# A decode kernel whose second FFN matrix is loaded on 96 + 32 partitions without repeated rows

## The chip, the cores and the metric

The kernel runs on one core of a Trainium2 chip. The metric is the device time of one execution in microseconds (us); smaller is better. A core has a tensor engine (PE, with its weight loads listed as PEld), a vector engine (DVE), a scalar engine (ACT), GpSimd (POOL), and a queue engine (SP) that does nothing but ask for transfers. Data lie in HBM, are moved by 16 DMA engines into SBUF (128 partitions), and matrix products arrive in PSUM (128 partitions, 8 banks of 512 float32 each).

## What is computed

One decode step for two sequences (B = 2, one token each), all in bfloat16: cached attention with 32 heads of 128 over 4096 keys, and beside it a feed-forward network (FFN) with a ReLU; a gate mixes the two.

```python
def reference(A_x, A_k_cache, A_v_cache, A_wq, A_wo, B_x, B_w1, B_w2, gate_w):
    x = A_x                                                  # [2, 1, 512]
    g = sigmoid((x * gate_w).sum(-1, keepdims=True))
    q = heads(x @ A_wq)                                      # 32 heads of 128
    scores = einsum("bhqd,bhkd->bhqk", q, A_k_cache) * 128 ** -0.5
    o = einsum("bhqk,bhkd->bhqd", softmax(scores), A_v_cache)
    a = merge(o) @ A_wo                                      # [2, 1, 512]
    h = maximum(einsum("bsd,df->bsf", x, B_w1), 0)           # w1 [512, 1376]
    b = einsum("bsf,fd->bsd", h, B_w2)                       # w2 [1376, 512]
    return g * a + (1 - g) * b
```

K and V have 64 MB each, `wq` and `wo` 4 MB each, `w1` and `w2` 1.4 MB each. Every byte is used once.

## The kernel before

**Queues and order.** The order of each engine's instructions is written out by hand: `pe(...)`, `dve(...)`, `act(...)`, `pool(...)` and `sp(...)` append an instruction to an engine's list; `waits` name the marks of other instructions (`signal`), `dwaits` a transfer's semaphore. All large loads go through SP, one after another, onto one queue: `w1` (line 264), `wq` (265), ten segments of K (269), V in seven units and two halves (274, 277, 280), `wo` in two parts (282, 283) and `w2` in six (284 and 288). SP waits ahead of an issue until the buffer that it fills is free.

**The stages.** `gate` transposes x, which then lies in `xT3` as [128, 4, 2] (partition p holds the elements 4p to 4p+3 of the 512), and works out the gate; `gm` is 1 - g. `q_proj` makes q with x at rest: `xTw` is the stationary operand, 32 columns wide, and `wq` moves, 512 columns at a time, in four column groups of the array (`tile_position=(0, 32 * (n % 4))`), so that results lie on the partitions 0, 32, 64 and 96 of the banks 5 and 6 (line 331). `ffn_h` follows. Then 64 pieces of K pass through `k_turn` (a block transposition of 32x32 on the DVE, line 384, into one of three buffers of `kt`) and `k_scores` (lines 405 and 197). `softmax` and `spread` make the weights; `v_unit` multiplies with V (line 458), `v_extract` and `o_gather` collect the heads.

**h.** `ffn_h` (line 363) makes h with w1 at rest: 44 matmuls (11 tiles of 128 columns of w1, 4 parts of the sum), each loading a 128x128 piece of w1 as weights and moving the 2 columns of x. Tile ft < 10 takes every tenth column of the first 1280, so that h number 10 p + ft comes to partition p, and tile 10 takes the columns 1248 to 1375. Two DVE instructions (line 373) apply the ReLU and the gate and write `hT` [128, 11, 2]. The first 32 entries of tile 10 are there twice, so POOL sets them to zero (line 377). `w1` lies in the memory of the first buffers of `kt`, and the first `k_turn` waits for the last of these matmuls.

**w2.** `w2f` is [128, 5632] in bfloat16, 11 rows of 512 for each partition. Row r < 10 on partition p is row 10 p + r of w2 (line 235); row 10 holds the rows 1248 to 1375, 32 of which are loaded twice (line 284). The five pieces of line 288 are column ranges of the rest: rows 0 to 4, 5 to 7, 8, and the two halves of 9. They go to the memory of the softmax's `E`, so the first of the six waits until the last `spread` is over.

**The end.** `project` multiplies with `wo` (line 504) in four column groups; the sums of the groups are copied by the DVE into `YW` (line 507). `fin(g)` is where the end result grows, 2 rows of 128 columns in each of the four column groups. `ffn_f(10, first=True)` starts this sum; `wo_sum` (line 526) adds the attention's part; `ffn_f(0)` to `ffn_f(8)` (line 512) add h times w2 row by row, each waiting for its piece of w2; `ffn_last(9)` does the last row with its weights already loaded (lines 202 and 208). DVE and ACT copy the result out (564, 566), and SP and ACT send it (291).

Of the kernel before, what the change touches and what calls it, by code (L numbers as in the profile page):

```python
# [3 lines left out]
dt = mybir.dt  # L4
# [6 lines left out]
DFF = 1376  # L11
# [74 lines left out]
def bass_gated_mix__gqa_block_cached__dense_activation_relu__decode_kernel(  # L86
# [14 lines left out]
    sb = nc.alloc_sbuf_tensor  # L101
# [4 lines left out]
    xT3 = sb("xT3", [128, 4, 4], dt.bfloat16)  # L106
# [26 lines left out]
    O_sb = sb("O_sb", [32, 2, 128], dt.bfloat16)  # L133
    oW = sb("oW", [128, 32, 2], dt.bfloat16)
    hT = sb("hT", [128, 11, 2], dt.bfloat16)
    out_sb = sb("out_sb", [2, 512], dt.bfloat16)


# [2 lines left out]
    w1 = flat[:, 0:2752].bitcast(dt.bfloat16)  # L141
    E = flat[:, 0:2048].bitcast(dt.bfloat16)
    ET = flat[:, 4096:6144].bitcast(dt.bfloat16)
    w2f = flat[:, 0:2816].bitcast(dt.bfloat16)
    w2 = w2f.rearrange("p (r n) -> p r n", n=512)
# [5 lines left out]
    PSF = nc.alloc_psum_tensor("PS", [128, 4096], dt.float32)  # L151
    PSB = PSF[:, :].bitcast(dt.bfloat16)

    def psf(p0, p1, c0, n):
        return PSF[p0:p1, c0:c0 + n]

    BANK = 512
    QR_B = 5
# [8 lines left out]
    H_C0 = MISC + 72  # L167
# [7 lines left out]
    sem = {n: nc.alloc_semaphore("sem_" + n) for n in names}  # L175
# [12 lines left out]
    def adder(engine):  # L188
        def add(fn, waits=(), signal=None, dwaits=()):
            P.add(engine, fn, waits=[marker(w) for w in waits], signal=marker(signal) if signal else None, dwaits=dwaits)  # L190
        return add

    pool, dve, act, pe, sp = (adder(e) for e in ("pool", "dve", "act", "pe", "sp"))
# [7 lines left out]
    def load_at(e, weights, g):  # L201
        return e.add_instruction(mybir.InstLdweights(
            tile_size=(128, 32), tile_position=(0, 32 * g), name=nc.get_next_instruction_name(), engine=mybir.EngineType.PE,
            ins=[e.lower_ap(weights)], outs=[]))

    def held_at(e, out, lhsT, rhs, g):
        low = e.lower_ap
        return e.add_instruction(mybir.InstMatmult(  # L208
            start_tensor_calc=False, stop_tensor_calc=True, tile_size=(128, 32), tile_position=(0, 32 * g), ldweights=False,
            name=nc.get_next_instruction_name(), engine=mybir.EngineType.PE, ins=[low(rhs), low(lhsT)], outs=[low(out)]))  # L210
# [5 lines left out]
         waits=["c_i16z"], signal="c_i16")  # L216
# [5 lines left out]
         waits=["c_i32z"], signal="c_i32")  # L222
# [6 lines left out]
         waits=["c_s4z"], signal="c_s4")  # L229
# [2 lines left out]
    wq_in = A_wq.rearrange("(p t) n -> p (t n)", t=4)  # L232
    w1_in = B_w1.rearrange("(p t) f -> p (t f)", t=4)
    wo_in = A_wo.rearrange("(p r) n -> p (r n)", r=32)
    w2_in = B_w2[0:1280, :].rearrange("(p r) n -> p (r n)", r=10)
    k_rows = A_k_cache.rearrange("b h s d -> (b h s) d")
    v_rows = A_v_cache.rearrange("b h s d -> (b h s) d")

# [20 lines left out]
    def place(g):  # L259
        return (4, 0, 2)[g % 3]  # L260
# [5 lines left out]
    for g, (u, halves) in enumerate(segments):  # L266
        dst = kv[:, 4, :] if len(halves) == 1 else region[:, place(g) // 2, :]
        src = unit_in(k_rows, u)[:, 16384 * halves[0]:16384 * (halves[-1] + 1)]
        sp(lambda e, g=g, dst=dst, src=src: e.dma_start(dst, src).then_inc(sem_k[g % 3], 16),
           waits=([f"kt_{last_of[g - 3]}"] if g >= 3 else ["pe_qr1"] if g == 2 else []))  # L270
    for u in range(7):
        if u == 2:
            for hf, dst, w in ((0, kv[:, 4, :], "kt_63"), (1, kv[:, 0, :], "pe_v_0")):
                sp(lambda e, hf=hf, dst=dst: e.dma_start(dst, unit_in(v_rows, 2)[:, 16384 * hf:16384 * (hf + 1)]).then_inc(sem_v[2 - 2 * hf], 16),
                   waits=[w])
            continue
        sp(lambda e, u=u: e.dma_start(region[:, u % 2, :], unit_in(v_rows, u)).then_inc(sem_v[u % 2], 16),
           waits=([f"pe_v_{u - 2}"] if u >= 2 else [f"kt_{last_of[7]}"] if u == 0 else [f"kt_{last_of[8]}"]))
    for hf in range(2):
        sp(lambda e, hf=hf: e.dma_start(kv[:, 2 + hf, :], unit_in(v_rows, 7)[:, 16384 * hf:16384 * (hf + 1)]).then_inc(sem_v[1 + hf], 16),  # L280
           waits=(["pe_v_5"] if hf == 0 else []))
    sp(lambda e: e.dma_start(wo_sb[:, 0:12288], wo_in[:, 0:12288]).then_inc(sem["wo0"], 16), waits=["pe_v_2"])
    sp(lambda e: e.dma_start(wo_sb[:, 12288:16384], wo_in[:, 12288:16384]).then_inc(sem["wo1"], 16))
    sp(lambda e: e.dma_start(w2[:, 10, :], B_w2[1248:1376, :]).then_inc(sem["w2a"], 16),
       waits=[f"pt_7_{hq}" for hq in range(4)])

    for name, c0, c1 in (("w2b", 0, 2560), ("w2c", 2560, 4096), ("w2d", 4096, 4608), ("w2e", 4608, 4864), ("w2f", 4864, 5120)):
        sp(lambda e, name=name, c0=c0, c1=c1: e.dma_start(w2f[:, c0:c1], w2_in[:, c0:c1]).then_inc(sem[name], 16))

    def send(b):  # L290
        return lambda e: e.dma_start(out.rearrange("b s n -> (b s) n")[b:b + 1, :], out_sb[b:b + 1, :]).then_inc(sem["out"], 16)
# [69 lines left out]
                waits=(["pe_q", "c_qbuf"] if g < 2 else [f"pe_sc_{last_of[g - 2]}"]), signal=f"q_{g}_{hq}")  # L361

    def ffn_h():
        for ft in range(11):
            for t in range(4):
                def fn(e, ft=ft, t=t):
                    o = t * DFF
                    cols = w1[:, o + ft:o + 1280:10] if ft < 10 else w1[:, o + 1248:o + 1376]
                    return e.matmul(psf(0, 128, H_C0 + 2 * ft, 2), lhsT=cols, rhs=xT3[:, t, 0:2], start=(t == 0), stop=(t == 3))
                pe(fn, dwaits=([(sem["w1"], 16)] if ft == 0 and t == 0 else []),  # L370
                   signal=("pe_h" if ft == 10 and t == 3 else None))
        for b in range(2):
            dve(lambda v, b=b: v.tensor_scalar(out=hT[:, :, b], in0=PSF[:, H_C0 + b:H_C0 + 22:2], scalar1=0.0,
                                               scalar2=gm[:, b:b + 1], op0=ALU.max, op1=ALU.mult),
                waits=["pe_h", "dve_gm"], signal=f"dve_h{b}")

        pool(lambda g: g.memset(hT[0:32, 10, :], 0.0), waits=["dve_h0", "dve_h1"], signal="c_h10")

    def k_turn(i):
        g, u, hf, h, rr = pieces[i]  # L380
# [116 lines left out]
    def fin(g):  # L497
        return psf(32 * g, 32 * g + 2, FIN_B * BANK, 128)

    def project():  # L500
        for r in range(32):
            dw = [(sem["wo0"], 16)] if r == 0 else [(sem["wo1"], 16)] if r == 24 else []
            t = r % 4
            pe(lambda e, r=r, t=t: e.matmul(psf(32 * t, 32 * t + 2, WO_B * BANK, 512), lhsT=oW[:, r, :], rhs=wo_sb[:, 512 * r:512 * r + 512],  # L504
                                            start=(r < 4), stop=(r >= 28), tile_position=(0, 32 * t)),
               dwaits=dw, waits=(["dve_oW0", "dve_oW1", "dve_z"] if r == 0 else []), signal=("pe_wo" if r == 31 else None))
        dve(lambda v: v.tensor_copy(out=YW, in_=psf(0, 128, WO_B * BANK, 512)), waits=["pe_wo"], signal="dve_yw")

    def ffn_f(r, first=False, signal=None):
        dw = {10: [(sem["w2a"], 16)], 0: [(sem["w2b"], 16)], 5: [(sem["w2c"], 16)], 8: [(sem["w2d"], 16)]}.get(r, [])  # L510
        for g in range(4):
            pe(lambda e, g=g: e.matmul(fin(g), lhsT=hT[:, r, :], rhs=w2[:, r, 128 * g:128 * g + 128],
                                       start=first, stop=(signal is not None), tile_position=(0, 32 * g)),
               dwaits=(dw if g == 0 else []), waits=(["dve_h0", "dve_h1", "c_h10", "dve_z"] if first and g == 0 else []),
               signal=(signal if g == 3 else None))

    def ffn_last(r):
        for g in range(4):
            pe(lambda e, g=g: load_at(e, hT[:, r, :], g))
        for g in range(4):  # L520
            pe(lambda e, g=g: held_at(e, fin(g), hT[:, r, :], w2[:, r, 128 * g:128 * g + 128], g),
               dwaits=([(sem["w2f" if g else "w2e"], 16)] if g % 2 == 0 else []), signal=(f"pe_fin{g // 2}" if g % 2 else None))

    def wo_sum():
        for g in range(4):
            pe(lambda e, g=g: e.matmul(fin(g), lhsT=selw[:, :], rhs=YW[:, 128 * g:128 * g + 128],
                                       start=False, stop=False, tile_position=(0, 32 * g)),
               waits=(["dve_yw", "dve_selw0"] if g == 0 else []))

    gate()  # L530
    selectors()
# [1 line left out]
    q_put(0)  # L533
    q_put(1)
    ffn_h()
    for i in range(64):
        k_turn(i)
# [15 lines left out]
            o_gather(0, [3])  # L553
    o_gather(1, [0, 1, 2, 3])
    project()
    ffn_f(10, first=True)
    wo_sum()
    for r in range(9):
        ffn_f(r)
    ffn_last(9)  # L560
    for c in range(4):
        dst, src = out_sb[:, 128 * c:128 * c + 128], fin(c)
        if c % 2 == 0:
# [36 lines left out]
```

## Time and profile before

| | |
|---|---|
| time, median of 3 runs | 344.48 us (344.44 to 344.49) |
| the profiled execution | 344.46 us |
| its span in the profile | 343.2 us |
| PE / PEld / DVE / ACT / POOL busy | 58 / 16 / 51 / 7 / 6% of the span |
| read from HBM | 145.46 MB, 424 GB/s over the span |
| `ffn_h` on PE (line 369) | 2.56 us from 22.67 us on |
| first transposition of K (line 384) | 25.91 us |
| `project` on PE (line 504) | 3.17 us from 335.05 us on |
| last matmul, sends | 340.9 to 341.2 us, 341.8 us |

The span is what the profiler records between the first and the last instruction; the execution's time has 1.3 us more around it. The profile gives for each engine the busy time, for each source line the instructions with their mean duration and what ended the idle time before them, for the DMA queues the packets and bytes, and a chain of waits: the work that ended last, followed back step by step to what released it. "DMA share" is the mean busy share of the 16 DMA engines.

### The profile page before, as it was taken

To read this page: it belongs to the slowest core of one execution; us is meant where nothing else is said; L and a number is where in the kernel's file an instruction comes from. 1 tells how busy PE (TensorE), PEld (TensorE's weight loads), DVE (VectorE), ACT (ScalarE), POOL (GpSimd) and SP (SyncE) were. 2 spreads that over 40 slices of the span, in tenths; PEclk is the share of its full clock that TensorE was granted. 3 is DMA by queue.
4 is the path that set the end of the run, shared out by engine and by line. 5 is a ranking of instruction groups with operands and counts; after the bars stand their busy time and mean duration, and the time that the engine had idled before them with its cause. 6 is when DMAs were issued, how large, how long until landed. Compare 5 with 4: busy or idle time off the path is not lost.

```text
span 343.2 us, 2528 instructions
## 1 busy us (share of the span) xinstructions
PE 200.1 (58%) x1226; PEld 53.4 (16%) x970; DVE 176.6 (51%) x124; ACT 22.8 (7%) x70; POOL 19.6 (6%) x34
## 2 busy tenths in 40 slices
PE   0167429799969799699799337423080503306455
PEld 0141001111111111111111012200030201102121
DVE  2239059899789899698999562202001030201021
ACT  1040000000000000000000240000000000000000
POOL 8000000000000000000000041101000010100000
PEclk9985858999989999989999856865558575856568
DMA  8998989899998999998999989999999999899996
GB/s 348 428 489 369 481 374 481 378 477 428 422 489 367 429 443 466 392 466 382 475 428 428 468 382 424 441 466 413 443 413 445 435 420 474 384 420 443 428 400 236
DMA packets 4340, 145.61 MB, mean 424 GB/s; under 512 B 485, under 2 KB 1002, under 8 KB 1258
## 3 DMA queue, kind: packets, MB, share of 16 engines
q1 hardware_dynamic: 4322, 145.46, 98.5%
q8 instruction: 8, 0.13, 0.2%
q14 instruction: 2, 0.02, 0.0%
q10 hardware_dynamic: 8, 0.00, 0.0%
HBM read 145.46 MB, written 0.00 MB: 424 GB/s over the span
## 4 chain that ended last, share of the span: by engine, by line
DMA 67%; DVE 19%; PE 11%; ACT 1%; issue 1%; POOL 0%; SPq 0%; DVEq 0%
DMA kv<-in_A_k_cache_dram 31%; DMA kv<-in_A_v_cache_dram 19%; DVE kt L384 16%; DMA kt<-in_B_w_dram 12%; PE PS L458 7%; DMA kv<-in_A_wq_dram 4%; ACT kt L426 1%; PE PS L405 1%; PE PS L197 1%; PE PS L331 1%; DVE mpad L411 1%; DVE kt L468 1%; POOL ptm L440 0%; DVE qbuf L464 0%; DVE kt L430 0%
## 5 line engine op out<-in xcount | busy, mean ns | idle before, releaser
L384 DVE STREAM_TRANSPOSE kt<-kv 128x2048 f32<-128x2048 f32 x64 | 141.2, 2274 | 22.7 <-DMA kv<-in_A_k_cache_dram 22.7
L405 PE MATMUL PS<-kt,qbuf 128*128 128x512 bf16 x256 | 107.0, 418 | 30.4 <-DVE kt L384 25.3
L197 PE MATMUL PS<-kt,qbuf 128*128 128x512 bf16 x256 | 106.5, 416 | 0.0
L458 PE MATMUL PS<-kv,ptm 128*32 128x512 bf16 x512 | 48.7, 559 | 77.3 <-DMA kv<-in_A_v_cache_dram 73.8
L464 DVE TENSOR_TENSOR qbuf<-PS,maskc 128x512 f32<-128x512 f32 x8 | 5.5, 692 | 111.4 <-PE PS L458 111.4
L405 PEld LDWEIGHTS PS<-kt,qbuf 128*128 128x128 bf16 x256 | 25.8, 101 | 139.9 <-issue 71.4
L458 PEld LDWEIGHTS PS<-kv,ptm 128*32 128x32 bf16 x512 | 18.7, 131 | 106.0 <-issue 85.4
L440 POOL COPY ptm<-kt 32x512 bf16<-32x512 bf16 x16 | 11.2, 697 | 259.2 <-DVE rsum L472 175.9
L358 ACT ACTIVATE qbuf<-PS 32x8 bf16<-32x8 bf16 x40 | 7.8, 196 | 134.3 <-PE PS L197 133.0
L444 ACT ACTIVATE ptm<-kt 32x512 bf16<-32x512 bf16 x8 | 5.1, 653 | 90.0 <-PE PS L458 88.7
L468 DVE TENSOR_REDUCE kt<-qbuf 128x128 f32<-128x512 f32 x8 | 8.2, 1029 | 0.3
L426 ACT ACTIVATE kt<-PS,negm 128x512 bf16<-128x512 f32 x8 | 5.4, 697 | 30.4 <-DVE negm L422 30.4
L331 PE MATMUL PS<-kv,xTw 128*32 128x512 bf16 x32 | 3.6, 631 | 5.9 <-DMA kv<-in_A_wq_dram 5.9
L475 PE MATMUL PS<-rsum,sell 128*32 128x1 f32 x4 | 0.4, 197 | 10.1 <-DVE rsum L472 10.1
L430 DVE STREAM_TRANSPOSE kt<-kt 128x1024 bf16<-128x1024 bf16 x4 | 5.0, 1245 | 1.7 <-ACT kt L426 1.4
L346 DVE CAST qrow<-PS 128x256 bf16<-128x256 f32 x2 | 2.4, 1397 | 6.4 <-PE PS L331 6.4
L298 PE MATMUL PS<-ident,x_sb 3*128 3x3 bf16 x4 | 0.3, 166 | 6.2 <-DMA x_sb<-in_gate_w_dram 6.2
L504 PE MATMUL PS<-kv,oW 128*2 128x512 bf16 x32 | 3.2, 570 | 0.9 <-DMA kv<-in_A_wo_dram 0.9
L566 ACT ACTIVATE out_sb<-PS 2x128 bf16<-2x128 f32 x2 | 0.5, 270 | 45.8 <-PE PS L208 45.7
L301 DVE COPY xT<-PS 128x12 bf16<-128x12 bf16 x1 | 0.2, 169 | 6.5 <-PE PS L298 6.5
L230 POOL MEMSET ptm<- 128x4096 bf16 x1 | 3.5, 3502 | 0.0
L411 DVE TENSOR_REDUCE mpad<-PS 128x1 f32<-128x2048 f32 x1 | 2.3, 2293 | 2.2 <-PE PS L197 2.2
(64 smaller groups left out, 44.2 us busy)
## 6 DMA issues: line engine op xcount, KB each, us to landing
kv<-in_A_k_cache_dram SPq DMA_DIRECT2D x4, 4096.0 KB, 31.6
kv<-in_A_v_cache_dram SPq DMA_DIRECT2D x4, 4096.0 KB, 27.3
kv<-in_A_wq_dram SPq DMA_DIRECT2D x1, 4096.0 KB, 15.0
kv<-in_A_wo_dram SPq DMA_DIRECT2D x1, 3072.0 KB, 39.3
kt<-in_B_w_dram SPq DMA_DIRECT2D x1, 1376.0 KB, 5.8
kv<-in_A_wo_dram SPq DMA_DIRECT2D x1, 1024.0 KB, 41.3
kt<-in_B_w_dram SPq DMA_DIRECT2D x1, 640.0 KB, 42.0
kt<-in_B_w_dram SPq DMA_DIRECT2D x1, 384.0 KB, 42.4
```

The costliest lines, as they stand in the source:

```text
L197: return e.add_instruction(mybir.InstMatmult(start_tensor_calc=start, stop_tensor_calc=stop, tile_size=(128, 128), tile_position=(0, 0), l ...
L331: pe(lambda e, n=n, t=t: e.matmul(psf(32 * (n % 4), 32 * (n % 4) + 32, (QR_B + n // 4) * BANK, 512), lhsT=xTw[:, t, :], rhs=wq_sb[:, t, n ...
L358: act(lambda a, hq=hq: a.activation(out=qbuf[32 * hq:32 * hq + 32, g % 2, :, :, 32 + 32 * hq], in_=cols[32 * hq:32 * hq + 32, u4 // 2, 2 * ...
L384: dve(lambda v: v.transpose(out=dst, in_=pairs[:, h, 64 * rr:64 * rr + 64]), waits=([f"pe_sc_{i - NKT}"] if i >= NKT else ["pe_h"] if i == ...
L405: return e.matmul(args[0], lhsT=args[1], rhs=args[2], start=first, stop=last)
L411: dve(lambda v: v.tensor_reduce(out=mpad[:, 0:1], in_=psf(0, 128, 0, 2048), axis=AX.X, op=ALU.max), waits=["pe_sc_63", "c_mpad"], signal=" ...
L426: act(lambda a, bk=bk, e2=e2: a.activation(out=blocks[:, bk, :, 16 * e2:16 * e2 + 16], in_=psf(0, 128, bk * BANK, 512).rearrange("p (r n) ...
L440: pool(lambda e, args=args: e.tensor_copy(**args), waits=waits, signal=f"pt_{u}_{hq}")
L444: act(lambda e, args=args: e.activation(func=ACT.Copy, **args), waits=waits, signal=f"pt_{u}_{hq}")
L458: pe(lambda e, m=m, t=t, at=at: e.matmul(psf(32 * t, 32 * t + 32, V_B[u % 2] * BANK, 512), lhsT=ptm[:, u % 2, 4 * m:4 * m + 4, :, :], rhs= ...
L464: dve(lambda e: e.tensor_tensor(out=Y.rearrange("p (c d) -> p c d", c=4), in0=psf(0, 128, V_B[u % 2] * BANK, 512).rearrange("p (c d) -> p ...
L468: dve(lambda e: e.tensor_reduce(out=X2[:, u, :], in_=Y.rearrange("p (c d) -> p d c", c=4), axis=AX.X, op=ALU.add), waits=[f"dve_y{u}"], si ...
```

## The change

h is made with x at rest and w1 moving; w2 is loaded with no row twice. The partitions 0 to 95 hold 11 rows of w2 each (1056 rows), the partitions 96 to 127 hold 10 each (320 rows).

`ffn_h` issues 16 matmuls: for each of the 4 parts of the sum, four column groups, each moving 352 columns of w1 (320 in the last group). Group g's result lies on the partitions 32 g and 32 g + 1 of bank 5. One block transposition on the DVE reads [128, 352] from PSUM, sees it as 11 blocks of 32 columns (every eleventh column to a block), and writes `hrow` [128, 11, 32], where partition p holds h number 11 p + r for both sequences. The two ReLU instructions read `hrow`. The memset on POOL is gone.

Of w2, the first load puts the ten rows of the partitions 96 to 127 in place; the other five load the partitions 0 to 95: rows 5 to 10, 2 to 4, 1, and the two halves of row 0. The sum now begins with `wo_sum`, and the rows follow from 10 (on 96 partitions) down to 0.

```diff
+    hrow = sb("hrow", [128, 11, 32], dt.float32)
...
-    w2_in = B_w2[0:1280, :].rearrange("(p r) n -> p (r n)", r=10)
+    w2_in = B_w2[0:1056, :].rearrange("(p r) n -> p (r n)", r=11)
+    w2_in2 = B_w2[1056:1376, :].rearrange("(p r) n -> p (r n)", r=10)
...
-    sp(lambda e: e.dma_start(w2[:, 10, :], B_w2[1248:1376, :]).then_inc(sem["w2a"], 16),
+    sp(lambda e: e.dma_start(w2f[96:128, 0:5120], w2_in2).then_inc(sem["w2a"], 16),
        waits=[f"pt_7_{hq}" for hq in range(4)])
-    for name, c0, c1 in (("w2b", 0, 2560), ("w2c", 2560, 4096), ("w2d", 4096, 4608), ("w2e", 4608, 4864), ("w2f", 4864, 5120)):
-        sp(lambda e, name=name, c0=c0, c1=c1: e.dma_start(w2f[:, c0:c1], w2_in[:, c0:c1]).then_inc(sem[name], 16))
+    for name, c0, c1 in (("w2b", 2560, 5632), ("w2c", 1024, 2560), ("w2d", 512, 1024), ("w2e", 0, 256), ("w2f", 256, 512)):
+        sp(lambda e, name=name, c0=c0, c1=c1: e.dma_start(w2f[0:96, c0:c1], w2_in[:, c0:c1]).then_inc(sem[name], 16))
...
     def ffn_h():
-        for ft in range(11):
-            for t in range(4):
-                def fn(e, ft=ft, t=t):
-                    o = t * DFF
-                    cols = w1[:, o + ft:o + 1280:10] if ft < 10 else w1[:, o + 1248:o + 1376]
-                    return e.matmul(psf(0, 128, H_C0 + 2 * ft, 2), lhsT=cols, rhs=xT3[:, t, 0:2], start=(t == 0), stop=(t == 3))
+        for t in range(4):
+            for g in range(4):
+                def fn(e, g=g, t=t):
+                    n = 11 if g < 3 else 10
+                    cols = w1[:, t * DFF + 352 * g:t * DFF + 352 * g + 32 * n].rearrange("p (a r) -> p a r", r=n)
+                    dst = psf(32 * g, 32 * g + 2, QR_B * BANK, 352).rearrange("p (a r) -> p a r", r=11)[:, :, 0:n]
+                    return e.matmul(dst, lhsT=xT3[:, t, 0:2], rhs=cols, start=(t == 0), stop=(t == 3), tile_position=(0, 32 * g))
...
+        dve(lambda v: v.transpose(out=hrow[:, :, :], in_=psf(0, 128, QR_B * BANK, 352).rearrange("p (a r) -> p r a", r=11)),
+            waits=["pe_h"], signal="dve_hr")
         for b in range(2):
-            dve(lambda v, b=b: v.tensor_scalar(out=hT[:, :, b], in0=PSF[:, H_C0 + b:H_C0 + 22:2], scalar1=0.0,
+            dve(lambda v, b=b: v.tensor_scalar(out=hT[:, :, b], in0=hrow[:, :, b], scalar1=0.0,
                                                scalar2=gm[:, b:b + 1], op0=ALU.max, op1=ALU.mult),
-                waits=["pe_h", "dve_gm"], signal=f"dve_h{b}")
-        pool(lambda g: g.memset(hT[0:32, 10, :], 0.0), waits=["dve_h0", "dve_h1"], signal="c_h10")
+                waits=["dve_hr", "dve_gm"], signal=f"dve_h{b}")
...
-        dw = {10: [(sem["w2a"], 16)], 0: [(sem["w2b"], 16)], 5: [(sem["w2c"], 16)], 8: [(sem["w2d"], 16)]}.get(r, [])
+        dw = {10: [(sem["w2a"], 16), (sem["w2b"], 16)], 4: [(sem["w2c"], 16)], 1: [(sem["w2d"], 16)]}.get(r, [])
+        k = 96 if r == 10 else 128
         for g in range(4):
-            pe(lambda e, g=g: e.matmul(fin(g), lhsT=hT[:, r, :], rhs=w2[:, r, 128 * g:128 * g + 128],
+            pe(lambda e, g=g: e.matmul(fin(g), lhsT=hT[0:k, r, :], rhs=w2[0:k, r, 128 * g:128 * g + 128],
...
-    ffn_f(10, first=True)
     wo_sum()
-    for r in range(9):
+    for r in range(10, 0, -1):
         ffn_f(r)
-    ffn_last(9)
+    ffn_last(0)
```

More of the change, by code (lines that the diff above doesn't have):

```diff
@@ L363, in ffn_h @@
     def ffn_h():
-        for ft in range(11):
-            for t in range(4):
-                def fn(e, ft=ft, t=t):
-                    o = t * DFF
-                    cols = w1[:, o + ft:o + 1280:10] if ft < 10 else w1[:, o + 1248:o + 1376]
-                    return e.matmul(psf(0, 128, H_C0 + 2 * ft, 2), lhsT=cols, rhs=xT3[:, t, 0:2], start=(t == 0), stop=(t == 3))
-                pe(fn, dwaits=([(sem["w1"], 16)] if ft == 0 and t == 0 else []),
-                   signal=("pe_h" if ft == 10 and t == 3 else None))
+        for t in range(4):
[5 more added lines that the diff above has]
+                    return e.matmul(dst, lhsT=xT3[:, t, 0:2], rhs=cols, start=(t == 0), stop=(t == 3), tile_position=(0, 32 * g))
+                pe(fn, dwaits=([(sem["w1"], 16)] if g == 0 and t == 0 else []),
+                   signal=("pe_h" if g == 3 and t == 3 else None))
+        dve(lambda v: v.transpose(out=hrow[:, :, :], in_=psf(0, 128, QR_B * BANK, 352).rearrange("p (a r) -> p r a", r=11)),
+            waits=["pe_h"], signal="dve_hr")
         for b in range(2):
-            dve(lambda v, b=b: v.tensor_scalar(out=hT[:, :, b], in0=PSF[:, H_C0 + b:H_C0 + 22:2], scalar1=0.0,
+            dve(lambda v, b=b: v.tensor_scalar(out=hT[:, :, b], in0=hrow[:, :, b], scalar1=0.0,
                                                scalar2=gm[:, b:b + 1], op0=ALU.max, op1=ALU.mult),
-                waits=["pe_h", "dve_gm"], signal=f"dve_h{b}")
-        pool(lambda g: g.memset(hT[0:32, 10, :], 0.0), waits=["dve_h0", "dve_h1"], signal="c_h10")
+                waits=["dve_hr", "dve_gm"], signal=f"dve_h{b}")
     def k_turn(i):
@@ L507, in project, with ffn_f @@
         dve(lambda v: v.tensor_copy(out=YW, in_=psf(0, 128, WO_B * BANK, 512)), waits=["pe_wo"], signal="dve_yw")
-    def ffn_f(r, first=False, signal=None):
-        dw = {10: [(sem["w2a"], 16)], 0: [(sem["w2b"], 16)], 5: [(sem["w2c"], 16)], 8: [(sem["w2d"], 16)]}.get(r, [])
+    def ffn_f(r):
+        dw = {10: [(sem["w2a"], 16), (sem["w2b"], 16)], 4: [(sem["w2c"], 16)], 1: [(sem["w2d"], 16)]}.get(r, [])
+        k = 96 if r == 10 else 128
         for g in range(4):
[L512 to L515, printed above, removed]
+            pe(lambda e, g=g: e.matmul(fin(g), lhsT=hT[0:k, r, :], rhs=w2[0:k, r, 128 * g:128 * g + 128],
+                                       start=False, stop=False, tile_position=(0, 32 * g)),
+               dwaits=(dw if g == 0 else []), waits=(["dve_h0", "dve_h1"] if r == 10 and g == 0 else []))
     def ffn_last(r):
@@ L526, in wo_sum @@
             pe(lambda e, g=g: e.matmul(fin(g), lhsT=selw[:, :], rhs=YW[:, 128 * g:128 * g + 128],
-                                       start=False, stop=False, tile_position=(0, 32 * g)),
-               waits=(["dve_yw", "dve_selw0"] if g == 0 else []))
+                                       start=True, stop=False, tile_position=(0, 32 * g)),
+               waits=(["dve_yw", "dve_selw0", "dve_z"] if g == 0 else []))
     gate()
```

## The prediction, made before the result was known

> **What bounds the kernel now.** I read the page first: the share of the DMA queues beside that of the engines.
>
> ```profile
> span 343.2 us, 2528 instructions
> ...
> PE 200.1 (58%) x1226; PEld 53.4 (16%) x970; DVE 176.6 (51%) x124; ACT 22.8 (7%) x70; POOL 19.6 (6%) x34
> ...
> q1 hardware_dynamic: 4322, 145.46, 98.5%
> q8 instruction: 8, 0.13, 0.2%
> ```
>
> No engine is busy for more than 58% of the span; the one queue that carries every load keeps the 16 DMA engines busy for 98.5% of it. So the end comes when the last byte has come, plus a short tail. The chain of waits, in order of time, shows which bytes these are:
>
> ```profile
> 297.88 42.44 DMA kt<-in_B_w_dram
> ...
> 340.36 0.34 PE PS L512 x12
> ...
> 340.73 0.23 PE PS L512 x4
> 340.96 0.20 PE PS L208 x2
> ...
> 341.18 0.28 DVE out_sb L564
> ```
>
> The pieces of w2 are asked for 42 us ahead and stand in the queue behind V and wo; L512 takes each piece as it lands. This is the stage that the change rebuilds. Two more views of it: the DMA answer for 337.0 to 343.2 us, in 40 slices of 0.155 us,
>
> ```profile
> DMA  9999999999978566545464300000000000000000
> GB/s 363 476 390 390 377 423 443 363 403 330 420 258 301 218 244 238 221 169 182 169 182 139 103 0 0 0 0 0 0 0 0 0 0 0 0 7 7 0 0 0
> ```
>
> and a table of windows of one microsecond, whose last two columns are the DMA share and GB/s:
>
> ```profile
> 338.00:339.00 1.00, 0.28 (x10) 0.00 (x0) 0.69 (x1) 0.00 (x0) 0.00 (x0) 1.00 0.94 346
> 339.00:340.00 1.00, 0.85 (x28) 0.37 (x28) 0.00 (x0) 0.00 (x0) 0.00 (x0) 1.00 0.58 215
> 340.00:341.00 1.00, 0.61 (x18) 0.25 (x20) 0.00 (x0) 0.00 (x0) 0.00 (x0) 1.00 0.27 82
> ```
>
> The rate does not stop at once: it sinks from about 420 GB/s to 100 between 338.6 and 340.5 us. Some of the 16 engines have finished their share while others are still at it; the idle part of 338 to 341 us is 0.06 + 0.42 + 0.73 = 1.2 us per engine on the mean, so the first and the last are some 1.5 to 2 us apart. A likely reason, inferred only, is the q8 row: 8 fetches of 16 KB of program, 0.2% of 16 engines' span, which is 11 us or about 1.4 us each, each holding up one engine.
>
> **The change, part by part.**
>
> *Fewer bytes and packets.* Before, w2 comes as 1280 + 128 = 1408 rows of 1 KB, 32 of them twice; after as 1056 + 320 = 1376. That is 32 KB less. The rate of this stretch: L512 starts on r = 0 at 339.44 us (w2b is there) and on r = 5 at 340.36 (w2c, 384 KB): 393 KB (thousands) in 0.92 us, 427 GB/s. So the bytes are worth 0.08 us. The small pieces are dearer per byte: w2d, 128 KB, comes 0.37 us after w2c where 427 GB/s would take 0.31; 0.06 us more for 128 packets, 8 to an engine. After the change, w2 is 32 + 5 x 96 = 512 packets, before 768: 16 fewer to each engine, so 2 x 0.06 = 0.12 us, taken as 0.10 because the big pieces show less. Sum: **-0.18 us**, on the path that sets the end.
>
> *Where the bytes go.* Every large load of the trace goes to all 128 partitions. In the new order w2a puts 320 KB into partitions 96 to 127 alone, and then w2b to w2f put 1056 KB into 0 to 95 alone. The trace shows no load of this kind, so I bound it. Lower bound: the rate doesn't depend on the partitions, and it costs nothing. Upper bound: a partition takes no more than the trace ever gives one, 438 GB/s (the window from 100 to 200 us) over 128, 3.42 GB/s. Then w2a takes 10,240 B / 3.42 = 2.99 us in place of 328 KB / 438 = 0.75, so 2.24 more; w2b to w2f take 11,264 / 3.42 = 3.29 us in place of 1081 KB / 438 = 2.47, so 0.82 more; together **+3.06 us**. That holds if all engines do w2a together and then w2b together. But they are 1.5 to 2 us apart here: while the late ones fill 96 to 127, the early ones already fill 0 to 95, and what overlaps isn't lost, since the two parts together fill every partition evenly (10 and 11 KB). Taking off the 1.5 us leaves **+1.55 us**, and that is the value I take, because nothing in the trace shows a partition that takes data faster and the out-of-step end is plain to see.
>
> [...]
>
> *The tail behind the last byte.* L512 for r = 10 ran under the DVE copy L507 (338.28 to 338.97 us); now it comes behind `wo_sum` and the landing of w2b. Twenty of these matmuls took 0.45 us (339.44 to 339.89), so six rows take 0.54 us, and 288 KB of w2c after it need 288 x 1.024 / 427 = 0.69 us: hidden. Rows 4 to 2 take 0.27 us against 0.23 us for the 96 KB of w2d, 0.04 over, gone again by w2f. If PE were always late, it would cost 0.1 us. `ffn_last`, the copies and the sends stay as they are: 0.
>
> *h.* These are rows of the timeline, and one of L331, which has the new form (x at rest, four column groups) for q:
>
> ```profile
> 16.23 3.64 PE L331 MATMUL PS<-kv,xTw 128*32 128x512 bf16 x32 [5.91 <-DMA kv<-in_A_wq_dram]
> ...
> 22.67 2.56 PE L369 MATMUL PS<-xT,kt 128*128 128x2 bf16 x44
> ...
> 25.91 8.89 DVE L384 STREAM_TRANSPOSE kt<-kv 128x2048 f32<-128x2048 f32 x4 [0.28 <-DMA kv<-in_A_k_cache_dram]
> ```
>
> 44 matmuls and 2.56 us go. 16 come, of 352 columns: 3.64 / 32 x 16 = 1.82 us at most, 1.25 scaled by columns, so h is there at 24.0 to 24.6 us instead of 25.2. The block transposition is new on the DVE: 128x32 took 0.21 us (L413) and 128x2048 2.27 us (L384), so 128x352 is 0.21 + 320 x 2.06 / 2016 = 0.54 us; reading PSUM with a stride could make it as slow as the cast L346, 1.40 us for 256 elements, 1.9 us. The two L373 keep their 0.37 (they began at 25.27). The DVE is free for the first L384 at 24.9 to 26.9 us, against 25.9 when K lands: 0 to 1.0 us late. What hides even the 1.0: L384 releases the next K issue (L269), and 8 MB of K took 30.7 us from issue to landing where 433 GB/s needs 19.4, so 11 us of other loads stand ahead. Without that cover it would cost up to 1.0 us. The POOL memset L377 (0.09 us) and its wait go, worth nothing, as nothing near waited. SP's issues stay six for w2 with the same single wait.
>
> Sum: 344.46 us (this execution; its span of 343.2 and 1.3 around it; the median of the runs is 344.48) - 0.18 + 1.55 + 0 + 0 = 345.83, so **345.9 us**.
>
> **Rivals.**
>
> *A, the partitions don't matter* (not slower): 344.46 - 0.18 = 344.3 us. For it: each of the 16 engines runs at 438 / 16 = 27 GB/s whatever it loads, and nothing in this trace shows that the far side sets that. Against it: nothing shows more than 3.42 GB/s into a partition either, and w2a at full rate asks for 427 / 32 = 13. It decides if w2b lands no later than before.
>
> *B, in step, or on fewer engines*: the 32 rows queue up in full, +3.06 - 0.18, 347.3 us. A spread of w2a over 4 engines gives the same, since 328 KB at 4 x 27 GB/s is 3.0 us. For it: of two engines held up equally the shift doesn't help. Against it: the sinking rate above. [...]
>
> *C, fewer instructions*: 28 matmuls with their weight loads fewer on PE, 56 instructions, may save one of the 8 program fetches. If that were the one that the last engine waits for, the end would come up to 1.4 us sooner: 342.9 us with the bytes. Against it: the other fetches leave other engines equally late, so one saved moves nothing.
>
> **How the numbers follow.** About 0.2% (0.7 us) is what a measurement of this kernel can tell from no change. The forecast, the overlap leaving 0.9 to 2.4 us of the 3.06 (345.2 to 346.7 us), has 0.55; B 0.16; A 0.24; C 0.05. Slower is the forecast and B, 0.71; same is A, 0.24; faster is C, 0.05. The range from 344.2 to 347.2 us takes in A, whose chance is too large to leave out, and leaves out C and the top of B. The forecast's own range is 345.2 to 346.7.
>
> **What would show it.** Right: bytes read fall by 32 KB and the packets by some 256; in the last 5 us the GB/s fall well under 420 while DMA share stays high, from the landing of wo on; w2b lands 1 us or more later; L512 for r = 10 waits on the DMA for it; everything before 335 us stands where it did within 0.3 us; h is ready at or before 25.9 us. Wrong: the GB/s hold at 420 up to the sinking end (A); a first L384 later than 26.9 us, or a gap in the DMA row before 300 us (the cover is gone); or late landings of V or wo, which the change doesn't touch.

## The result, and the profile after

The changed kernel takes 347.19 us (median of 6 runs, 346.87 to 347.27), the kernel before 344.49 us (344.44 to 344.64): a ratio of 1.0076, interval 1.0065 to 1.0086, 2.70 us slower. The profiled execution took 346.96 us, its span 345.7.

The pages, the lines that count what the queue moved. First one line of the kernel before, then the changed kernel:

```profile
DMA packets 4340, 145.61 MB, mean 424 GB/s; under 512 B 485, under 2 KB 1002, under 8 KB 1258
```

```profile
span 345.7 us, 2472 instructions
...
DMA packets 4084, 145.58 MB, mean 421 GB/s; under 512 B 485, under 2 KB 778, under 8 KB 970
...
q1 hardware_dynamic: 4066, 145.43, 98.4%
q8 instruction: 8, 0.13, 0.2%
```

The change does what it says: 256 packets fewer (4340 before) and 0.03 MB less on q1 (145.46 before). The queue is as busy as ever, and the span is 2.5 us longer. The end of the chain of waits, changed kernel (start, duration, what):

```profile
298.13 44.05 DMA kt<-in_B_w_dram
342.18 0.14 issue
342.31 1.24 PE PS L518 x31
343.55 0.13 PE PS L209 x2
343.68 0.03 issue
343.70 0.28 DVE out_sb L568
```

L518 is the old L512. It starts on w2b at 342.31 us, where it started on its w2b at 339.44 before, by this row of the timeline of the kernel before:

```profile
339.44 0.26 PEld L512 LDWEIGHTS PS<-kt,hT 128*2 128x2 bf16 x20 [0.31 <-DMA kt<-in_B_w_dram]
```

What follows is no longer than it was. Two windows of one microsecond of the kernel before, which the prediction doesn't show, and then the windows of the changed kernel (the last three columns are PE clock, DMA share, GB/s):

```profile
336.00:337.00 1.00, 1.00 (x16) 0.28 (x8) 0.00 (x0) 0.00 (x0) 0.00 (x0) 0.50 0.94 375
337.00:338.00 1.00, 1.00 (x16) 0.31 (x12) 0.00 (x0) 0.00 (x0) 0.00 (x0) 0.66 1.05 412
```

```profile
336.00:337.00 1.00, 1.00 (x12) 0.15 (x4) 0.00 (x0) 0.00 (x0) 0.00 (x0) 0.50 0.93 227
337.00:338.00 1.00, 0.13 (x4) 0.00 (x0) 0.00 (x0) 0.00 (x0) 0.00 (x0) 0.50 1.12 258
338.00:339.00 1.00, 0.00 (x0) 0.00 (x0) 0.00 (x0) 0.00 (x0) 0.00 (x0) 0.50 0.91 209
339.00:340.00 1.00, 0.93 (x8) 0.10 (x8) 0.00 (x0) 0.00 (x0) 0.00 (x0) 0.50 0.94 216
340.00:341.00 1.00, 0.20 (x8) 0.11 (x8) 0.69 (x1) 0.00 (x0) 0.00 (x0) 0.50 1.02 218
341.00:342.00 1.00, 0.49 (x8) 0.00 (x0) 0.00 (x0) 0.00 (x0) 0.00 (x0) 0.50 0.62 198
```

The loss is in this view. From 336 to 341 us the DMA engines are as busy as before (shares near 1), but they move 209 to 258 GB/s where the kernel before moved 375 and 412 in the first two of these windows. Busy is not the same as moving: in the packet records of the trace the packets take longer (the 3 KB packets of w2c 173 ns on the mean, 124 before). The 32 packets of w2a, 10 KB each, took 654 ns on the mean, and the fastest of them 391. Whether they wait on the far side, at the partitions, is what the experiments test. The same stretch in the DMA answer for 337.0 to 345.7 us, slices of 0.22 us:

```profile
DMA  7994977987999999889646654530000000000000
GB/s 198 292 264 104 405 179 174 301 203 155 212 226 254 235 287 186 158 174 247 195 127 243 235 200 163 163 111 17 0 0 0 0 0 0 0 0 0 9 0 0
```

The last data come in slice 28, at about 343.1 us, 2.6 us ahead of the end of the span; before it was slice 23 of 0.155 us, 340.6 us, also 2.6 us ahead. So the tail behind the last data hasn't changed.

One row shows that not only w2 is late. The second part of `wo` stands ahead of w2 in the queue and goes to all 128 partitions, as before. First the kernel before, then the changed one, the weight load that waits for it (rows of the timeline):

```profile
337.48 0.22 PEld L504 LDWEIGHTS PS<-kv,oW 128*2 128x2 bf16 x8 [0.63 <-DMA kv<-in_A_wo_dram]
```

```profile
339.07 0.10 PEld L509 LDWEIGHTS PS<-kv,oW 128*2 128x2 bf16 x8 [2.87 <-DMA kv<-in_A_wo_dram]
```

It is 1.6 us later, though `project` began at the same time (335.04 us). The DMA engines that had finished their share of `wo` were already writing w2a to partitions 96 to 127 (its first packet starts at 334.83 us, the last packet of `wo` ends at 338.10), and the others' remaining packets of `wo` became slower: in the packet records, the 8 KB packets of this load took 313 ns on the mean before and 384 ns after, up to 627.

### The profile page after: what moved, and what is told of

Same layout as the page of the kernel before. It is cut to its first block, busy times and chain, and to the rows that moved or that the text cites. A ratio compares the mean times of both kernels' runs of the same rounds, so it can differ in the third digit from the quotient of the medians.

```text
span 345.7 us, 2472 instructions
## 1 busy us (share of the span) xinstructions
PE 197.0 (57%) x1198; PEld 51.4 (15%) x942; DVE 177.1 (51%) x125; ACT 22.9 (7%) x70; POOL 19.5 (6%) x33
## 4 chain that ended last, share of the span: by engine, by line
DMA 77%; DVE 11%; PE 11%; issue 0%; SPq 0%; DVEq 0%
DMA kv<-in_A_k_cache_dram 31%; DMA kv<-in_A_v_cache_dram 29%; DMA kt<-in_B_w_dram 13%; DVE kt L389 10%; PE PS L463 5%; DMA kv<-in_A_wq_dram 4%; PE PS L410 3%; PE PS L198 2%; PE PS L334 1%; PE PS L518 0%; DVE kt L473 0%; DVE qbuf L469 0%; DVE out_sb L568 0%; SPq L267 0%; DVE ptm L447 0%
## 5 line engine op out<-in xcount | busy, mean ns | idle before, releaser
L463 PE MATMUL PS<-kv,ptm 128*32 128x512 bf16 x512 | 45.6, 530 | 80.5 <-DMA kv<-in_A_v_cache_dram 79.3
L512 DVE COPY qbuf<-PS 128x512 f32<-128x512 f32 x1 | 0.7, 692 | 5.7 <-PE PS L509 5.7
```

The lines of the kernel that those rows point to most:

```text
L463: pe(lambda e, m=m, t=t, at=at: e.matmul(psf(32 * t, 32 * t + 32, V_B[u % 2] * BANK, 512), lhsT=ptm[:, u % 2, 4 * m:4 * m + 4, :, :], rhs= ...
```

## The experiments

All differences are against the kernel before, measured beside each group of runs on the same chip (344.52 us for e1 to e4, 344.40 for t0 to t3, 344.42 for the others). The 95% interval of each difference is about 0.3 to 0.6 us to either side. The theories: **loads** (where the bytes of w2 go) against **engines** (the new h); and, within the loads, a **cap** on each partition (the prediction's upper bound), **half the rate** (half of 438 GB/s for a narrow load, a supposition that no run had shown), or neither.

**Which half of the change costs.** Two kernels, each with half of it:

```diff
 e1, against the kernel before (hrow and the whole of ffn_h as changed)
-            waits=(["dve_h0", "dve_h1", "c_h10", "dve_z"] if first and g == 0 else []),
+            waits=(["dve_h0", "dve_h1", "dve_z"] if first and g == 0 else []),
 e2, against the changed kernel (the whole of ffn_h, with its memset, as before)
-            waits=(["dve_h0", "dve_h1"] if r == 10 and g == 0 else []))
+            waits=(["dve_h0", "dve_h1", "c_h10"] if r == 10 and g == 0 else []))
```

> The new way of making h (x at rest, one block transposition) with the loads of w2 and the order of the sum as before; h then meets other rows of w2 than its own. Theory 'loads' (the 2.7 us come from where the bytes of w2 go): as before, 344.3 to 344.6 us. Theory 'engines' (the new h or its transposition holds something up): 345 us or more.

> The new loads of w2 and the new order of the sum with h made as before; h then meets other rows of w2 than its own. Theory 'loads': as after the change, 346.9 to 347.3 us. Theory 'engines': 344.3 to 345 us.

e1: 344.53 us, ratio 1.0001 (0.9992 to 1.0011). e2: 347.15 us, 1.0078 (1.0061 to 1.0094). The loads have all of it, and the new h costs nothing that can be measured. Why, in rows of the changed kernel's timeline:

```profile
22.96 1.34 PE L374 MATMUL PS<-kt,xT 128*2 128x352 bf16 x16
...
24.35 0.55 DVE L377 STREAM_TRANSPOSE hrow<-PS 128x352 f32<-128x352 f32 x1 [3.70 <-PE PS L374]
24.94 0.38 DVE L380 TENSOR_SCALAR hT<-hrow,gm 128x11 bf16<-128x11 f32 x2
25.91 6.70 DVE L389 STREAM_TRANSPOSE kt<-kv 128x2048 f32<-128x2048 f32 x3 [0.60 <-DMA kv<-in_A_k_cache_dram]
```

The matmuls take 1.34 us (2.56 before), the transposition 0.55, and the DVE then waits 0.60 us for K. The gain of 1.2 us on PE and the transposition's cost both vanish in that wait.

**Which loads.** One narrow part at a time, the other on 128 partitions. Both edits are against the changed kernel; in e3, `w2x_in` is rows 0 to 1023 of w2, eight to a partition, and the column ranges of the five loads are fitted to it:

```diff
 e3
-        sp(lambda e, name=name, c0=c0, c1=c1: e.dma_start(w2f[0:96, c0:c1], w2_in[:, c0:c1]).then_inc(sem[name], 16))
+        sp(lambda e, name=name, c0=c0, c1=c1: e.dma_start(ET[:, c0:c1], w2x_in[:, c0:c1]).then_inc(sem[name], 16))
...
 e4
-    w2_in2 = B_w2[1056:1376, :].rearrange("(p r) n -> p (r n)", r=10)
+    w2_in2 = B_w2[1056:1376, :].rearrange("r n -> (r n)").rearrange("(p c) -> p c", p=128)
...
-    sp(lambda e: e.dma_start(w2f[96:128, 0:5120], w2_in2).then_inc(sem["w2a"], 16),
+    sp(lambda e: e.dma_start(ET[:, 0:1280], w2_in2).then_inc(sem["w2a"], 16),
```

> After the change, but only w2a (320 KB) goes to partitions 96 to 127 alone; the other five loads bring 1024 KB to all 128 partitions, into memory that the matmuls do not read, so the FFN's part of the result is not w2's. Bytes and packets alone: 64 KB and 96 packets less than before, -0.2 us, 344.3. Partitions capped at 3.42 GB/s each and nothing overlapping: 2.24 more, 346.5 us. Half the rate for 32 partitions: 0.75 more, 345.0 us. Rate independent of partitions: 344.3 us.

> After the change, but w2a's 320 KB go to all 128 partitions (2.5 KB each, into memory that the matmuls do not read), and the other five loads to partitions 0 to 95 as after the change. [...] Rate independent of partitions: 344.4 us. If this loss and that of the run with w2a alone on 32 partitions add up to the whole 2.7 us and some tenths for bytes, nothing of the two overlapped in the change; if they add up to clearly more, some of it did.

e3: 346.27 us, 1.75 more than before, ratio 1.0051 (1.0036 to 1.0065); with the 0.2 us that bytes and packets should give, w2a on 32 partitions costs 1.95 us. e4: 346.62 us, 2.10 more, 1.0060 (1.0045 to 1.0075); with 0.1 us, the five loads on 96 partitions cost 2.2. The cap had 0.82 for these: the larger miss is here. Together the two cost 4.15 us one by one, and 2.70 + 0.18 = 2.88 in the change, so about 1.3 us overlap, if the two are added up like this; with the intervals above it can be half a microsecond more or less. Two windows, e3 first and then e4, show the same sign as in the changed kernel, a DMA share of 1 at some 220 to 250 GB/s:

```profile
336.00:338.00 2.00, 1.68 (x16) 0.27 (x8) 0.00 (x0) 0.00 (x0) 0.00 (x0) 0.50 1.00 224
```

```profile
336.00:338.00 2.00, 1.79 (x20) 0.29 (x11) 0.00 (x0) 0.00 (x0) 0.00 (x0) 0.50 1.07 246
```

**Cap, half the rate or neither.** Into the kernel before, ahead of w2a, goes one load that nothing reads, with the same 512 KB in three shapes (and half of it in a fourth):

```diff
 t1 (t0: ET[:, 0:2048] and wo_in[:, 0:2048], t2: ET[32:96, :] and wo_in[32:96, 0:4096], t3: ET[96:128, :] and wo_in[96:128, 0:4096])
-    sp(lambda e: e.dma_start(w2[:, 10, :], B_w2[1248:1376, :]).then_inc(sem["w2a"], 16),
+    sp(lambda e: e.dma_start(ET[0:64, :], wo_in[0:64, 0:4096]).then_inc(sem["wx"], 16),
        waits=[f"pt_7_{hq}" for hq in range(4)])
+    sp(lambda e: e.dma_start(w2[:, 10, :], B_w2[1248:1376, :]).then_inc(sem["w2a"], 16))
...
```

> The kernel before with one load more, 512 KB that nothing reads, ahead of w2a: 4 KB to each of 128 partitions. All theories: 524 KB / 438 GB/s = 1.2 us more, 345.7 us. This is the yardstick for the next three.

> The same 512 KB to partitions 0 to 63, 8 KB each. Cap for each partition (3.42 GB/s): 2.4 us more than before, 346.9. [...] Rate independent of partitions: 345.7 us.

> The same 512 KB to partitions 32 to 95, 8 KB each: as many partitions as in the run before, only others. Cap for each partition: 346.9 us, no difference to partitions 0 to 63. [...] Rate independent of partitions: 345.7 us.

> 256 KB to partitions 96 to 127, 8 KB each, nothing reads them. At full rate 0.6 us more than before, 345.1. [...] Cap for each partition: 2.4 us more, 346.9 us.

| partitions | bytes | time | more than before |
|---|---|---|---|
| 0 to 127 | 512 KB | 345.76 us | 1.36 us, ratio 1.0038 (1.0023 to 1.0053) |
| 0 to 63 | 512 KB | 347.96 us | 3.56 us, 1.0106 (1.0091 to 1.0121) |
| 32 to 95 | 512 KB | 345.66 us | 1.26 us, 1.0037 (1.0024 to 1.0050) |
| 96 to 127 | 256 KB | 346.48 us | 2.08 us, 1.0063 (1.0046 to 1.0080) |

Sixty-four partitions are as good as 128 if they are 32 to 95 (1.26 us against 1.36), and 2.3 us worse if they are 0 to 63 (3.56). That ends the cap for each partition, and a rate that doesn't depend on partitions too. Why these two sets of 64 differ, no trace shows. Half the rate alone is too little for the two dear loads: it would give 2.4 us on 0 to 63, where 3.56 were measured, and 1.2 on 96 to 127, where it was 2.08. (The rows of `wo` that are read differ with the partitions; no run changes the one without the other.) The DMA answers for 334 to 344 us, slices of 0.25 us, first for partitions 0 to 63, then for 32 to 95:

```profile
DMA  5999999979779998989899897999898999876655
GB/s 229 426 426 459 426 295 262 229 164 262 197 172 324 213 299 180 299 193 299 176 209 238 160 254 119 139 168 168 176 311 332 410 373 428 318 283 264 231 211 180
```

```profile
DMA  8999999998999997999999998655551000000000
GB/s 361 459 393 459 426 393 459 393 426 348 385 459 377 410 463 295 377 418 446 406 369 385 397 350 301 238 217 197 168 156 49 0 0 0 0 0 0 0 0 8
```

The DMA engines are busy in both until the data run out. In the first the rate falls to about 215 GB/s, half of 438, for some six microseconds, longer than 524 KB / 219 GB/s = 2.4 us, and then comes back: packets of the loads around it are slow as well. (This profiled run of t1, 348.67 us, is the slowest of its four; the others took 347.73 to 348.18.) The packet records say it too: the 5 KB packets of w2b, which go to all partitions and stand behind this load, took 318 ns on the mean with it on 0 to 63, and 203 ns with it on 32 to 95.

**Engines in step.** Is the surplus over half the rate due to engines out of step, some 2 us apart at the end of the kernel (w2a lands from 335.87 to 337.78 us in the kernel before)? The same loads between the first and second segments of K, where they are together: the first segment of K landed on all 16 within 0.4 us in the kernel before. Two theories: the half rate and no more, 1.2 us for the bytes and 1.2 on top on partitions 0 to 63, 346.9 us; or the 2.3 us between the two loads on 64 partitions, wherever the load stands, 348.0 us.

```diff
 u1 (u2: ET[32:96, :] and wo_in[32:96, 0:4096], u3: ET[0:96, :] and wo_in[0:96, 0:4096])
+        if g == 0:
+            sp(lambda e: e.dma_start(ET[0:64, :], wo_in[0:64, 0:4096]).then_inc(sem["wx"], 16))
...
-            dwaits=([(sem_k[g % 3], 16 * (g // 3 + 1))] if i == first_of[g] else []), signal=f"kt_{i}")
+            dwaits=([(sem_k[g % 3], 16 * (g // 3 + 1))] if i == first_of[g] else [(sem["wx"], 16)] if i == 2 else []), signal=f"kt_{i}")
```

> The 512 KB that nothing reads go to partitions 0 to 63 again, but near the start of the kernel, between the first and the second segment of K, where the 16 engines are still in step (w1 lands on all of them within 0.4 us). [...]

> The same early place, partitions 32 to 95: 1.2 to 1.3 us for the bytes, 345.7 us by both theories. The yardstick for the other two.

> The same early place, 768 KB to partitions 0 to 95, 8 KB each: bytes 1.8 us, 346.2. [...] At the price that the five loads on 96 partitions had at the end (2.2 us for 1056 KB, so 1.6 on top): 347.8 us.

u1: 347.20 us, 2.78 more, ratio 1.0080 (1.0066 to 1.0093). u2: 345.54, 1.12 more, 1.0033 (1.0021 to 1.0045). u3: 347.67, 3.25 more, 1.0093 (1.0078 to 1.0109). Between 0 to 63 and 32 to 95 there are 1.66 us here and 2.30 at the end of the kernel; half the rate would be 1.2. So the place seems to add about 0.6 us, which would fit engines out of step, and some 0.4 us stay unexplained early on; but each of these two remainders lies within the intervals of the runs that it is taken from, so neither is shown. The third is the telling one: 786 thousand bytes in 3.25 us are 242 GB/s, nearer to half of 438 than to three quarters (329, what the cap gives 96 partitions). What the load costs beyond its bytes at full rate, 3.25 - 1.8 = 1.45 us, is about what u1 costs beyond its own, 2.78 - 1.2 = 1.58. By the cap it would have been 2.4 - 1.8 = 0.6. Of its 96 packets of 8 KB, 13 took under 340 ns, the others up to 732; in u2 all 64 took 309. So at least 19 of the 32 packets to partitions 64 to 95 are among the slow ones, although u2, which loads these partitions too, had none. That a packet merely waits behind a slow one of its own engine doesn't explain it: in the packet records, looked at every 0.25 us, 16 or 17 packets are open in this stretch, so each of the 16 engines has about one at a time. Which engine takes which rows the trace doesn't show, and why these packets are slow stays open.

**All rows once, without narrow loads.** Only the last 96 rows need fewer than 128 partitions, 64 of them on partitions 32 to 95 and 32 on 96 to 127:

```diff
-    sp(lambda e: e.dma_start(w2[:, 10, :], B_w2[1248:1376, :]).then_inc(sem["w2a"], 16),
+    sp(lambda e: e.dma_start(w2[32:96, 10, :], B_w2[1280:1344, :]).then_inc(sem["w2a"], 16),
        waits=[f"pt_7_{hq}" for hq in range(4)])
+    sp(lambda e: e.dma_start(w2[96:128, 10, :], B_w2[1344:1376, :]).then_inc(sem["w2a"], 16))
...
-        dw = {10: [(sem["w2a"], 16)], 0: [(sem["w2b"], 16)], 5: [(sem["w2c"], 16)], 8: [(sem["w2d"], 16)]}.get(r, [])
+        dw = {10: [(sem["w2a"], 32)], 0: [(sem["w2b"], 16)], 5: [(sem["w2c"], 16)], 8: [(sem["w2d"], 16)]}.get(r, [])
```

> [...] 32 KB and 32 packets less, -0.09 us; 32 KB at half the rate, or at the price measured for 256 KB on these partitions (1.5 us on top), +0.08 to +0.19. 344.4 to 344.6 us: no difference that can be measured. If any load on fewer than 128 partitions were dear in itself: 345 us or more.

f2: 344.37 us against 344.42, ratio 1.0000 (0.9991 to 1.0008): no difference that can be measured. The 32 KB that the change wanted to save are worth 0.08 us by the prediction's estimate, too little to see; no version here beats the kernel before. Nor does a load of 32 KB on 32 partitions cost anything that can be seen.

## Why the prediction was right or wrong

**Bytes and packets, -0.18 us.** The counts came as predicted (32 KB, 256 packets). No run shows the price: the 32 KB alone, saved in the last run, are lost in the measurement.

**h, nothing.** Right, by e1. The matmuls took 1.34 us (1.25 to 1.82 predicted), the transposition 0.55 (0.54; the slow reading of PSUM that the upper bound feared didn't come), and h was there at 25.3 us, ahead of K.

**Where the bytes go, +1.55 us.** The direction was right, and so was the kind of cause: the rate depended on which partitions a load went to (the same 512 KB added 3.56 us on 0 to 63 and 1.26 on 32 to 95), and what stands ahead of the last part of `wo` kept its time (`project` began at 335.04 us, 335.05 before). The size was off, 2.70 us slower where 1.4 were forecast, and the steps that gave it don't hold. The first is the cap of 3.42 GB/s for each partition, from which 2.24 and 0.82 us were worked out. It was the rate of loads that all go to 128 partitions, so it says what a partition was given there and not what it can take; partitions 32 to 95 took 8 KB each in 1.26 us more, 416 GB/s. The second is the term "w2b to w2f take 11,264 / 3.42 = 3.29 us ... so 0.82 more": 2.2 us were measured. The run on 96 partitions near the start came nearer to half the rate, at 242 GB/s. The first term came out as 1.95 us; the cap gave 2.24, which the interval of e3 doesn't exclude, and half the rate 0.75, which it does. The overlap was taken as 1.5 us, and 1.3 is what is left over when the whole is taken from the two parts, so no run measures it by itself.

**Luck.** The measured 347.19 us lies 0.01 us inside the upper end of the stated range (344.2 to 347.2). That is luck: the forecast's own range, 345.2 to 346.7 us, misses it by 0.5, and the wider one was set to take in rival A and a part of B, not a dearer load on 96 partitions.

**Out of step.** The prediction took this only as a relief. It was a cost as well: while engines that were ahead were on the narrow w2a, the packets of the others, still on a wide load, took longer (the 8 KB packets of `wo` 384 ns, 313 before). So `wo` came 1.6 us later, and w2a is enough for it: in e3, where w2a alone is narrow, these packets took 384 ns on the mean too. What the prediction only inferred of the reason, the program fetches, the trace of the kernel before bears out. At 25.5 us the last of the 16 engines to land its share of K is 0.4 us behind the first; after the fetch at 30.3 us one engine is 1.9 us behind; and after each of the other seven fetches one more of them lags, until ten of the sixteen do (two fell behind at other times). Why a fetch of 1.0 to 1.1 us leaves a lag of some 1.5 stays open.

**The tail.** Hidden, as predicted: the last data are 2.6 us ahead of the end in both.

**Rivals.** A (the partitions don't matter) is out by t1 against t2. B's figure, 347.3 us, was nearest, but not for its reason: its cap is out by the same two runs, and its spread of w2a over 4 engines is out because up to 10 packets of w2a are open at once. C (a program fetch less) is out: 8 fetches before and after. Its price was off too: a fetch took 1.0 to 1.1 us in the packet records, not the 1.4 that the rounded 0.2% gave.

## What to carry to other kernels

In a kernel that is bound by its loads, a few bytes less can be worth nothing if they narrow a large load: here 32 KB saved put more than a megabyte onto narrow loads and cost 2.70 us. Count which partitions a load reaches before counting its bytes, and keep each large load on all 128, or on 32 to 95, the one narrower range tried here that cost no more (1.26 us against 1.36). Narrow loads slowed their neighbours in the queue too (the 5 KB packets of w2b took 318 ns behind the load on 0 to 63, 203 behind that on 32 to 95), so look at the loads before and behind one. The sign was a DMA share near 1 beside GB/s at about half of 438: 209 to 258 in the changed kernel, 224 and 246 in e3 and e4, about 215 with the load on 0 to 63.

## What the runs showed of the hardware that was not expected

- Bytes over added time, near the start of the kernel: 242 GB/s on partitions 0 to 95, and 189 (524 / 2.78) on 0 to 63. At the end of the kernel: 416 (524 / 1.26) on 32 to 95 and 385 (524 / 1.36) on all 128. On 32 to 95 near the start the added time, 1.12 us, was no more than the 1.2 us of the full 438 GB/s.
- 256 KB on partitions 96 to 127 at the end of the kernel cost 2.08 us, more than the 1.2 of half the rate. Loads to all partitions around it became slower too (the 5 KB packets of w2b took 267 ns on the mean, 204 in the kernel before); how much of the 2.08 us this explains wasn't tried.
- The granted PE clock stayed at 0.50 from 336 to 345 us in the changed kernel, where it had been 1.00 from 338 us on before. The tail was no longer for it (2.6 us in both), and why the clock differs wasn't tried.
